# Weights on a second DMA queue, wider pixel loads, and a forward transform split in three frequency ranges, in a convolution kernel

## The chip, the cores and the metric

One NeuronCore of a Trainium2 chip. The metric is the device time of one execution in microseconds (us). Each experiment ran on one chip together with runs of the kernel before, and all comparisons below are of runs in the same (fast) state; only under e10 are its slow runs named too. The experiments ran on several chips, so across experiments the ratios to the kernel before are compared, not the times.

## The reference, cut to what matters

```python
def setup_inputs():
    H = W = 224; C = 96; K = 7
    return {"x": normal(1, H, W, C) * 0.05,      # bfloat16
            "w": normal(K, K, C, C) * 0.05}      # bfloat16

def reference(x, w):
    wp = jnp.pad(w, ((0, H - K), (0, W - K), (0, 0), (0, 0)))
    Xf = rfft2(x.astype(float32), axes=(1, 2))
    Wf = rfft2(wp.astype(float32), axes=(0, 1))
    Yf = jnp.einsum('bhwi,hwio->bhwo', Xf, Wf)
    return irfft2(Yf, s=(H, W), axes=(1, 2)).astype(bfloat16)
```

It is a circular 7x7 convolution of a 224x224 image with 96 channels in and out. The image wraps round, so the first columns need the six last ones; they are called the halo here.

## The kernel before

The kernel transforms along the height only. The 224 rows are cut into 8 blocks of 28, and each block with its 6 rows of overlap (34 rows) goes to 17 frequencies by a matmul with a matrix `Fm` that the kernel computes at its start (iotas, a sine on ScalarE, masks on GpSimd, a cast on VectorE). The width is worked through in 7 tiles of 32 columns, in the order: forward transform (xn by Fm gives xf), one *round* for each of the 17 frequencies (products with the transformed weights WF), inverse transform. Sums and differences of xf (the J buffers) save products. Two tiles run interleaved at first: tile 1 follows tile 0 with a lag of four rounds. The weights are transformed too (wq by Em gives WF): the first group, of two frequencies, in the head and the other five groups during the rounds.

All loads are issued by SyncE, in this order:

```python
load_rows(xh_bufs[0], 0, W - PAD, PAD)     # halo, rows of block group 0: 112 + 6 partitions, 6 pixels
load_x(0)                                  # 16 pixels, 112 + 6 partitions
load_rows(xh_bufs[1], 1, W - PAD, PAD)     # halo of group 1
load_x(1)
for h in range(2):
    if h:
        for c in range(2, NXN):            # NXN = 4 pixel buffers
            load_x(c)
    for p0, p1 in ((0, 48), (48, PW)):     # weights: 48 rows of 18,432 bytes, then the 49th
        dma(wq[h * PW + p0:h * PW + p1, 0:C * C - h * C2], wsrc[p0:p1, h * C2:])
```

ScalarE's program begins with the table load for the sine (a dummy activation), then the sine for Fm. PE warms its clock with 24 matmuls on zeros and then runs the head:

```python
a0 = a_jobs(0)                   # tile 0, whole forward: 12 halo matmuls + 64, all of 136 columns
p0 = prep_jobs(0)                # weights of frequencies 0 and 1: 96 matmuls of 50 columns
for _ in range(16): a0.pop(0)()
for _ in range(4):  p0.pop(0)()
while p0 or a0:                  # the two are mixed
    if p0: p0.pop(0)()
    for _ in range(2):
        if a0: a0.pop(0)()
...
for r in range(NS + LAG):        # rounds
    if r == 0:
        add(0, 2 * LAG - 2, a_jobs(1))   # tile 1's forward beside rounds 0 to 3, 136 columns
```

Each result in PSUM is evicted by ScalarE or VectorE, whichever a running account of their work says is less loaded.

## Time and profile before

| | before |
|---|---|
| median time | 291.92 us (290.88 to 292.42) |
| profiled span | 291.0 us |
| PE busy | 272.5 us, 94% |
| mean granted clock | 0.965 |
| first forward matmul | 8.74 us |
| first weight-transform matmul | 14.54 us |
| first product of round 0 | 26.43 us |
| start of the last group of weight transforms (round 16) | 82.56 us |

In the timeline a row gives the start of a group, its busy time, its engine and line, the operation, and in brackets the idle time before it with what ended it. "SPq" and "ACTq" are the sequencers of SyncE and ScalarE, with the DMA issues. Two things of the kernel before matter later. The first is when its sine runs; the second is that one load already waits. From the timeline of the head:

```profile
3.83 0.64 SPq L86 DMA_DIRECT2D wq<-in_w_dram  x2
5.39 0.41 ACT L86 ACTIVATE ct<-ct,ct 118x136 f32<-118x136 f32 x1 [3.10 <-DVE ct L86]
```

And from the waits of SyncE's queue in the first 40 us (sum of the waits, how many, longest):

```profile
SPq L86 <- DMA wq<-in_w_dram: 5.5, 2, 5.3
SPq L86 <- DMA xn<-in_x_dram: 2.9, 4, 0.9
```

The reader is to see that the sine waited for nothing but VectorE's arithmetic (5.39 us), and that SyncE stood 5.3 us in one wait on a load. SyncE has nothing else to do, so that wait cost nothing. I read it only as a sign of when the weights landed.

### The profile page before, as it was taken

The page shows a single profiled execution, that of the slowest core. Times are in us where ns is not written, and L with a number is a line of the kernel's source. Part 1 is how long each engine was busy: PE and PEld are TensorE (multiplying, and loading weights), DVE is VectorE, ACT ScalarE, POOL GpSimd, SP SyncE. Part 2 cuts the span into 40 slices and gives each one's busy share as a digit, 9 for nine tenths or more (in the row PEclk, how much of TensorE's full clock was granted, in tenths as well). Part 3 has the DMA queues.
Part 4 walks back from the last instruction along what each step waited for, and adds up shares of the span by engine and source line. Part 5 has one row for each costly group of instructions (what it writes and reads, how often), then busy time and mean ns, then how long its engine had stood idle before and what let it go on. Part 6 is the DMA issues. An engine that isn't in the chain of part 4 may idle for free.

```text
span 291.0 us, 11983 instructions
## 1 busy us (share of the span) xinstructions
PE 272.5 (94%) x5010; PEld 244.2 (84%) x5010; DVE 229.6 (79%) x472; ACT 195.8 (67%) x488; POOL 113.1 (39%) x151
## 2 busy tenths in 40 slices
PE   8598998999999998999899998999999999999982
PEld 3488988999999997888899987898988989888761
DVE  7847399997978889979977888787998779786723
ACT  2555994958774555886788867897788865677113
POOL 6824022348446565332643227222552323422100
PEclk9955899999999999999999999999999999999997
DMA  8894142111111299977567685778539543887756
GB/s 195 132 236 124 51 112 84 45 43 44 43 43 49 87 277 193 274 225 216 170 190 206 194 243 144 204 210 237 169 95 267 148 131 108 198 245 197 201 108 189
DMA packets 45830, 46.04 MB, mean 158 GB/s; under 512 B 33626, under 2 KB 34758, under 8 KB 45678
## 3 DMA queue, kind: packets, MB, share of 16 engines
q1 hardware_dynamic: 43488, 43.21, 55.3%
q10 hardware_dynamic: 2288, 2.06, 2.5%
q8 instruction: 39, 0.64, 1.0%
q14 instruction: 15, 0.12, 0.2%
HBM read 23.92 MB, written 21.33 MB: 156 GB/s over the span
## 4 chain that ended last, share of the span: by engine, by line
PE 65%; DVE 14%; DMA 5%; issue 5%; POOL 4%; ACT 4%; SPq 1%; DVEq 0%; ACTq 0%; POOLq 0%
PE pb L86 65%; DVE J L86 6%; POOL ct L86 3%; DVE v L86 2%; DMA tt<-scr 2%; DVE u L86 2%; DMA xf<-scrb 2%; ACT xf L86 2%; DVE WF L86 1%; DVE yf L86 1%; DVE ct L86 1%; ACT WF L86 1%; POOL yf L86 1%; SPq L86 1%; DMA scrb<-yf 1%
## 5 line engine op out<-in xcount | busy, mean ns | idle before, releaser
L86 PE MATMUL pb<-WF,J 96*128 96x96 bf16 x2898 | 169.2, 206 | 2.8 <-DVE J L86 1.4
L86 PEld LDWEIGHTS <-J 96*128 96x128 bf16 (+1 forms) x2910 | 142.9, 98 | 18.5 <-issue 10.1
L86 POOL TENSOR_TENSOR yf<-v,u 128x384 bf16<-128x384 f32 x85 | 83.7, 999 | 144.9 <-issue 97.3
L86 ACT CAST xf<-pb 96x408 bf16<-96x408 f32 (+3 forms) x150 | 68.4, 481 | 11.3 <-PE pb L86 9.2
L86 ACT CAST yo<-pb 84x384 bf16<-84x384 f32 (+1 forms) x144 | 61.4, 481 | 6.4 <-PE pb L86 3.4
L86 DVE TENSOR_TENSOR J<-xf 96x1824 bf16<-96x1824 bf16 (+1 forms) x84 | 64.4, 806 | 0.0
L86 PE MATMUL pb<-WF,xf 96*128 96x96 bf16 x952 | 60.7, 207 | 2.1 <-DVE WF L86 2.0
L86 PE MATMUL pb<-Fm,xn 118*128 118x136 bf16 (+3 forms) x576 | 52.1, 216 | 2.4 <-DVE u L86 1.9
L86 PEld LDWEIGHTS <-xf 96*128 96x128 bf16 x952 | 47.5, 98 | 2.6 <-issue 1.5
L86 PEld LDWEIGHTS <-xn 118*128 118x128 bf16 x576 | 34.3, 100 | 3.8 <-issue 2.9
L86 PE MATMUL pb<-tt,Gm 102*84 102x384 bf16 (+1 forms) x144 | 35.8, 329 | 0.6 <-DVE v L86 0.4
L86 ACT CAST WF<-pb 96x480 bf16<-96x480 f32 (+1 forms) x62 | 30.7, 570 | 5.1 <-PE pb L86 5.1
L86 PE MATMUL pb<-wq 98*128 98x120 bf16 (+1 forms) x336 | 26.5, 234 | 2.3 <-POOL ct L86 2.3
L86 DVE TENSOR_TENSOR J<-J 96x912 bf16<-96x912 bf16 (+1 forms) x42 | 28.3, 674 | 0.0
L86 PEld LDWEIGHTS <-wq 98*128 98x128 bf16 (+1 forms) x336 | 23.8, 152 | 3.8 <-POOL ct L86 2.4
L86 POOL COPY xf<-xf 96x816 bf16<-96x816 bf16 (+3 forms) x16 | 16.7, 1073 | 0.0
L86 DVE TENSOR_TENSOR yf<-v,u 128x384 bf16<-128x384 f32 x27 | 15.5, 575 | 0.9
L86 PEld LDWEIGHTS <-Gm 102*84 102x84 bf16 (+1 forms) x144 | 11.4, 114 | 3.1 <-issue 0.6
L86 PE MATMUL pb<-wu 128*112 128x384 bf16 (+1 forms) x60 | 13.0, 380 | 1.1 <-DVE ct L86 1.1
L86 PEld LDWEIGHTS <-wu 128*112 128x112 bf16 (+1 forms) x60 | 7.3, 124 | 6.4 <-issue 2.5
L86 DVE TENSOR_TENSOR WF<-WF 96x960 bf16<-96x960 bf16 x15 | 11.0, 787 | 0.1
L86 ACT CAST tt<-pb 112x384 bf16<-112x384 f32 x8 | 3.6, 479 | 9.7 <-PE pb L86 9.6
(388 smaller groups left out, 210.2 us busy)
## 6 DMA issues: line engine op xcount, KB each, us to landing
xn<-in_x_dram SPq DMA_DIRECT2D x28, 336.0 KB
scr<-yf SPq DMA_DIRECT2D x30, 288.0 KB
tt<-scr SPq DMA_DIRECT2D x24, 288.0 KB
out_dram<-yo SPq DMA_DIRECT2D x24, 252.0 KB
tt<-scr SPq DMA_DIRECT2D x12, 192.0 KB
out_dram<-yo SPq DMA_DIRECT2D x12, 168.0 KB
out_dram<-tt SPq DMA_DIRECT2D x4, 336.0 KB
scr<-yf SPq DMA_DIRECT2D x6, 192.0 KB
```

The costliest lines, as they stand in the source:

```text
L86: r = fn(*a, **k)
```

## The change

Its intent: start the weights at once, on ScalarE's queue, so that they don't stand behind the pixels; do only what round 0 needs of the forward transform in the head (frequencies 0 to 7 of 17), and push the other two ranges, and tile 1 in three ranges, into later rounds; keep PE's clock up with nine warming matmuls after the halo (17 stand at the start, where 24 did).

```diff
+    x0_bufs = [xn_bufs[0], J_bufs[2][0:R, 0:XW + 32]]        # 32-pixel buffers; tile 0's second in J
...
+    def load_w(h):
+        for p0, p1 in ((0, 48), (48, PW)):
+            SE.dma_start(out=wq[h * PW + p0:h * PW + p1, 0:C * C - h * C2], in_=wsrc[p0:p1, h * C2:])
+    load_w(0)
     load_rows(xh_bufs[0], 0, W - PAD, PAD)
-    load_x(0)
     load_rows(xh_bufs[1], 1, W - PAD, PAD)
-    load_x(1)
-    ... (weights and two more pieces on SyncE)
+    load_x(0, 0)
+    load_x(0, 1)
...
+    warm(8); warm(9)                     # instead of 24 warming matmuls
...
+    SE.copy(out=zw, in_=...)             # ScalarE zeroes the rest of wq, instead of GpSimd
...
-    VE.tensor_copy(out=Fm..., in_=qf[:]) # this cast comes ahead of the masks now
...
-    (head as above)
+    for jg in range(2):
+        for f in a_bank(0, xf0, xh_bufs[jg], 0, 3, jg, 0):   # halo: 12 matmuls
+            f()
+    warm(9)
+    load_x(1, 1)
+    fj = f_jobs(0, 0)                    # first range: 64 columns instead of 136
+    for f in fj[0]: f()
+    load_w(1)
+    for f in prep_jobs(0) + fj[1]: f()
...
-        add(2 * PGRP[gi - 1][0], 2 * PGRP[gi - 1][1] - 1, prep_jobs(gi))
+        add(2 * PGRP[gi - 1][0] + (gi == 1), 2 * PGRP[gi - 1][1] - (gi > 1), prep_jobs(gi))   # weights: group 1 a step later
...
-            add(0, 2 * LAG - 2, a_jobs(1))
+            f1, f2 = f_jobs(0, 1), f_jobs(0, 2)
+            add(0, 4, f1[0] + f2[0][:-1] + [then_load(f2[0][-1], 1, 0)] + f1[1] + f2[1])
+        for p in range(3):
+            if r == (1, 3, 5)[p]:        # tile 1's three ranges
+                new_xf(1, SH2[p], SH2[p + 1])
+                fj = f_jobs(1, p)
+                ...
+                add(2 * r + 1, 2 * r + (5, 5, 4)[p], fj[0] + fj[1])
```

More of the change, by code (lines that the diff above doesn't have):

```diff
@@ L40 @@
 CQ = {2: (12, 0), 3: (12, 2), 4: (10, 5), 5: (7, 8), 6: (4, 12)}
-NXN = 4
 SH2 = (0, 8, 13, 17)
@@ L143 @@
     assert sum(KB) == 128
-    xn_bufs = [cpool.tile([R, PXC * C + 32], BF16, name=f"xn{i}") for i in range(NXN)]
+    XW = 2 * TW * C
+    xn_bufs = [cpool.tile([R, XW + 32], BF16, name=f"xn{i}") for i in range(2)]
+    x0_bufs = [xn_bufs[0], J_bufs[2][0:R, 0:XW + 32]]
     wtmp_cm = tc.tile_pool(name="wtmp", bufs=1, side="right")
@@ L153 @@
     XHW = PAD * C + 32
-    xh_bufs = [J_bufs[2][0:R, i * XHW:(i + 1) * XHW] for i in range(2)]
-    for xb in xn_bufs:
-        GE.memset(xb[:, PXC * C:], 0.0)
+    xh_bufs = [xn_bufs[1][:, i * XHW:(i + 1) * XHW] for i in range(2)]
+    for xb in (xn_bufs[0], xn_bufs[1], x0_bufs[1]):
+        GE.memset(xb[:, XW:], 0.0)
     for xb in xh_bufs:
@@ L167, in load_rows, with xbuf, load_x @@
         ld(0, PAD, h0 % H)
-    def load_x(c):
-        t, k = divmod(c, 4)
-        h, jg = divmod(k, 2)
-        load_rows(xn_bufs[c % NXN], jg, t * 2 * TW + h * PXC, PXC)
+    def xbuf(t, jg):
+        return (xn_bufs if t else x0_bufs)[jg]
+    def load_x(t, jg):
+        load_rows(xbuf(t, jg), jg, t * 2 * TW, 2 * TW)
     wsrc = w.rearrange("kh kw i o -> (kh kw) (i o)")
-    NCH = 4 * NT
+    def load_w(h):
+        for p0, p1 in ((0, 48), (48, PW)):
+            SE.dma_start(out=wq[h * PW + p0:h * PW + p1, 0:C * C - h * C2], in_=wsrc[p0:p1, h * C2:])
+    load_w(0)
     load_rows(xh_bufs[0], 0, W - PAD, PAD)
-    load_x(0)
     load_rows(xh_bufs[1], 1, W - PAD, PAD)
-    load_x(1)
-    for h in range(2):
-        if h:
-            for c in range(2, NXN):
-                load_x(c)
-        for p0, p1 in ((0, 48), (48, PW)):
-            dma(wq[h * PW + p0:h * PW + p1, 0:C * C - h * C2], wsrc[p0:p1, h * C2:])
+    load_x(0, 0)
+    load_x(0, 1)
+    for xf in xf_bufs:
+        GE.memset(xf[0:C, :, :, NS - 1, POS - 1, :], 0.0)
     wu = cpool.tile([128, 128], BF16, name="wu")
@@ L189, with warm @@
     VE.memset(wu[:], 0.0)
-    for _ in range(3):
+    def warm(n):
         pwu = bank()
-        for _ in range(8):
+        for _ in range(n):
             TE.matmul(pwu[:].rearrange("p (a b) -> p a b", a=4), lhsT=wu[:, 0:128], rhs=wur, start=True, stop=True)
+    warm(8)
+    warm(9)
     ntmp = [0]
@@ L212 @@
     SE.activation(out=dmy[:], in_=pi_t[:], func=ACTF.Sin, bias=0.0, scale=0.0)
+    zw = wqx[0:PW2, C * C + 2 * NSLOT * NTAP:]
+    SE.copy(out=zw, in_=wu[0:PW2, 0:1].to_broadcast(list(zw.shape)))
     def sin_q(q):
@@ L230 @@
     iota(twc[:], [[1, KT]])
-    GE.memset(wqx[0:PW2, C * C + 2 * NSLOT * NTAP:], 0.0)
     VE.memset(a2[:, 0, 1:2], 34.0)
@@ L251 @@
     sin_q(qe[:])
+    VE.tensor_copy(out=Fm.rearrange("p r s j -> p j s r"), in_=qf[:])
     VE.tensor_scalar(out=mk[:, 0:KT], in0=twc[:], scalar1=twp[:, 0:1], scalar2=None, op0=ALU.is_equal)
@@ L255 @@
     VE.tensor_tensor(out=mk2[:, 0], in0=mk[:], in1=mk2[:, 1], op=ALU.subtract)
-    VE.tensor_copy(out=Fm.rearrange("p r s j -> p j s r"), in_=qf[:])
     pe3 = ftile([PW2, NSLOT])
@@ L395, in a_bank, with then_load, g @@
         return [pair] if t > 2 and NP2 else [single(0), single(1)]
+    def then_load(f, t, jg):
+        def g():
+            f()
+            if t < NT:
+                load_x(t, jg)
+        return g
     def a_jobs(t):
@@ L399, in a_jobs @@
         jobs = []
-        if t == 0:
-            for jg in range(2):
-                jobs.extend(a_bank(t, xf, xh_bufs[jg], 0, 3, jg, 0))
-        for k in range(4):
-            h, jg = divmod(k, 2)
-            c = 4 * t + k
-            for (q, n) in ((0, 3), (3, 3), (6, 2)):
-                jobs.extend(a_bank(t, xf, xn_bufs[c % NXN], 2 * q, n, jg, HALO + h * 8 + q))
-            last = jobs.pop()
-            def fin(last=last, c=c):
-                last()
-                if c + NXN < NCH:
-                    load_x(c + NXN)
-            jobs.append(fin)
+        for jg in range(2):
+            for h in range(2):
+                for (q, n) in ((0, 3), (3, 3), (6, 2)):
+                    jobs.extend(a_bank(t, xf, xn_bufs[jg], h * PXC + 2 * q, n, jg, HALO + h * 8 + q))
+            jobs.append(then_load(jobs.pop(), t + 1, jg))
         return jobs
@@ L427, in f @@
                 for k in range(b - a):
-                    h, i = divmod(2 * (a + k) + ph, PXC)
-                    xb = xn_bufs[(4 * t + 2 * h + jg) % NXN]
-                    TE.matmul(pa[:, k * n:(k + 1) * n], lhsT=xb[:, i * C:i * C + 128], rhs=fv, start=True, stop=True)
+                    i = 2 * (a + k) + ph
+                    TE.matmul(pa[:, k * n:(k + 1) * n], lhsT=xbuf(t, jg)[:, i * C:i * C + 128], rhs=fv, start=True, stop=True)
                 xo = xf_tiles[t][0:C, ph, :, s0:s1, HALO + a:HALO + b, jg * JG:(jg + 1) * JG]
@@ L434, in mk_ @@
             return f
-        return [mk_(jg, a, b, ph) for jg in range(2) for a, b in zip(e[:-1], e[1:]) for ph in range(2)]
+        return [[mk_(jg, a, b, ph) for a, b in zip(e[:-1], e[1:]) for ph in range(2)] for jg in range(2)]
     jbuf = {}
@@ L649, in queue_c @@
         pump()
-    a0 = a_jobs(0)
-    p0 = prep_jobs(0)
-    for _ in range(16):
-        a0.pop(0)()
-    for _ in range(4):
-        p0.pop(0)()
-    while p0 or a0:
-        if p0:
-            p0.pop(0)()
-        for _ in range(2):
-            if a0:
-                a0.pop(0)()
+    xf0 = new_xf(0)
+    for jg in range(2):
+        for f in a_bank(0, xf0, xh_bufs[jg], 0, 3, jg, 0):
+            f()
+    warm(9)
+    load_x(1, 1)
+    fj = f_jobs(0, 0)
+    for f in fj[0]:
+        f()
+    load_w(1)
+    for f in prep_jobs(0) + fj[1]:
+        f()
     for f in jit(0, 0):
@@ L706 @@
         if r == 0:
-            add(0, 2 * LAG - 2, a_jobs(1))
+            f1, f2 = f_jobs(0, 1), f_jobs(0, 2)
[4 more added lines that the diff above has]
+                fj = f_jobs(1, p)
+                if p == 2:
+                    for jg in range(2):
+                        fj[jg][-1] = then_load(fj[jg][-1], 2, jg)
+                add(2 * r + 1, 2 * r + (5, 5, 4)[p], fj[0] + fj[1])
         for p in range(3):
@@ L712 @@
                 if p == 2:
-                    for i in (1, 3):
-                        def fin(f=fj[i], i=i):
-                            f()
-                            for h in range(2):
-                                load_x(12 + 2 * h + i // 2)
-                        fj[i] = fin
-                add(2 * r, 2 * r + (8, 7, 5)[p], fj)
+                    for jg in range(2):
+                        fj[jg][-1] = then_load(fj[jg][-1], 3, jg)
+                add(2 * r, 2 * r + (8, 7, 5)[p], fj[0] + fj[1])
         if r == PGRP[-2][1] + 1:
```

## The prediction

> **What bounds the kernel now.** I read the page first: PE is busy 94% of the span, and the row of the granted clock shows one hole.
>
> ```profile
> PE   8598998999999998999899998999999999999982
> PEclk9955899999999999999999999999999999999997
> ```
>
> Each digit is a slice of 7.28 us. PE works in every slice after the head, but in slices 3 and 4 its clock is near one half. The diff touches the first two tiles only, so next I read the timeline of 0 to 45 us.
>
> ```profile
> 8.22 0.47 DVE L86 CAST Fm<-ct 118x136 bf16<-118x136 f32 x1
> 8.74 0.87 PE L86 MATMUL pb<-Fm,J 118*128 118x136 bf16 x12 [0.70 <-DVE ct L86]
> ...
> 14.32 28.73 SPq L86 DMA_DIRECT2D xn<-in_x_dram  x16
> 14.54 2.50 PEld L86 LDWEIGHTS <-wq 49*128 49x128 bf16 x40 [2.43 <-POOL ct L86]
> ...
> 18.51 0.86 PE L86 MATMUL pb<-Fm,xn 118*128 118x136 bf16 x6
> ...
> 19.30 0.71 PE L86 MATMUL pb<-wq 49*128 49x50 bf16 x8
> ...
> 26.43 0.80 PE L86 MATMUL pb<-WF,xf 96*128 96x96 bf16 x8 [0.75 <-DVE WF L86]
> ```
>
> Here the reader sees the head: the forward transform waits for the matrix Fm (8.7 us), the weight transform waits until 14.5 us, and the first product of the convolution comes at 26.4 us. The wait of 2.4 us before 14.54 is put down to GpSimd, but the only GpSimd write that those matmuls read, a memset, ended at 4.4 us. SyncE's queue was released at the same moment (14.32), and the waits of that queue name the weight DMA with 5.3 us. So I take it that the first half of the weights landed at about 14.2 us, although it was issued at 3.8, behind 0.97 MB of pixels.
>
> Then the windows of ten microseconds:
>
> ```profile
> 20.00:30.00 10.00, 9.25 (x98) 8.16 (x98) 7.01 (x10) 6.06 (x15) 3.02 (x3) 0.50 0.53 133
> 30.00:40.00 10.00, 9.68 (x156) 9.09 (x154) 5.30 (x10) 9.64 (x26) 0.00 (x0) 0.91 0.29 76
> 50.00:60.00 10.00, 10.00 (x217) 10.00 (x216) 9.22 (x19) 7.41 (x17) 4.64 (x5) 1.00 0.09 33
> ```
>
> The columns are PE, PEld, DVE, ACT, POOL, then clock, DMA share and GB/s. From 30 to 40 us ACT is full (9.64), from 50 us on PE is. I count rounds by the products on xf: round 1 starts at 33.4, 2 at 37.0, 3 at 42.2, 4 at 45.1 us. So there are three stages: a head to 26.4 us that waits and runs at half clock; rounds 0 to 3 (18.7 us) bound by ACT's evictions; and from round 4 on PE.
>
> Last, what a matmul costs in a dense stream, read from the starts of successive groups on PE:
>
> ```profile
> 69.65 0.40 PE L86 MATMUL pb<-Fm,xn 118*128 118x64 bf16 x8
> 69.88 0.93 PE L86 MATMUL pb<-WF,J 96*128 96x96 bf16 x18
> ...
> 76.98 0.92 PE L86 MATMUL pb<-wq 98*128 98x120 bf16 x12
> 77.73 0.40 PE L86 MATMUL pb<-Fm,xn 118*128 118x64 bf16 x8
> ...
> 89.57 0.36 PE L86 MATMUL pb<-Fm,xn 118*128 118x40 bf16 x8
> 89.78 1.16 PE L86 MATMUL pb<-WF,J 96*128 96x96 bf16 x18
> ...
> 108.04 0.34 PE L86 MATMUL pb<-Fm,xn 118*128 118x136 bf16 x3
> 108.22 0.33 PE L86 MATMUL pb<-WF,J 96*128 96x96 bf16 x4
> ```
>
> 77.73 - 76.98 over 12 is 62 ns for a weight transform; (89.78 - 89.57)/8 is 26 ns for 40 columns; (108.22 - 108.04)/3 is 60 ns for 136. (69.88 - 69.65)/8 is 29 ns for 64 columns, in a group that nothing stalls; 16 of 32 columns take 0.40 us, 25 ns. The weight transform took 62 ns at half clock too (2.50 us of weight loads for 40), so it is bound by its strided weight loads and not by the clock.
>
> **What the Trainium skill says.** "TensorE: Matmul & The Clock Gate", section "What's actually happening": PE is half rate by default, a busy window of 3413 ns frees it, an idle one throttles it, and windows run free. The trace agrees: weight loads of the warm-up come every 0.43 us to 4.4 us and every 0.21 after; the half clock lasts from about 14.6 to 31.7 us (from the 0.66 and 0.57 of two 2 us windows), 17.1 us or five such windows. It also shows that a busy PE isn't enough: the mixed stream of 14.6 to 28 us didn't bring the clock back. "DMA: Bandwidth & Descriptors", section "Issuing engines are not separate DMA queues": issuing from two engines "will only save the time on the sequencer". The same page, "Queues, rings and completion order": an engine takes turns between the queues' rows packet by packet. So ScalarE's queue adds no bandwidth, but the weights no longer stand behind the pixels. No trace of the kernel before shows two busy queues in the head.
>
> **The change part by part.**
>
> 1. *Fm.* Its cast moves ahead of the mask work on VectorE and can start near 7.5 instead of 8.22 us; two more GpSimd memsets cost about 0.15. First forward matmul at about 8.2 us: 0.5 gained.
>
> 2. *Weights on ScalarE's queue.* They now start at about 1 us with the halos. By 14.2 us the old head had moved some 2.3 MB, 190 GB/s. Weights (0.88 MB) and as much of the pixels at that rate, from 2 us on, is 11 us (estimate; I allow 9.5 to 13).
>
> 3. *Forward of tile 0 in the head.* Instead of 76 matmuls of 136 columns, 12 for the halo and 64 of 64 columns for the first range; 17 warming matmuls at first and 9 more after the halo. From 8.2 us: 12 x 60 ns = 0.7; 9 x 213 ns = 1.9 (the old warm-up's spacing); 32 x 29 ns = 0.9; 96 x 62 ns = 6.0; 32 x 29 ns = 0.9; last eviction and hop 0.8 as before. That sums to 11.2, so the first product comes at 19.4 us, and with half a microsecond for a late landing at 19.9. Against 26.4: **6.5 us gained**. The weights are wanted at 11.7 us, just after my estimate of their landing.
>
> 4. *Rounds 0 to 3.* Out go 24 evictions of tile 1 (16 of 408 columns at 0.48 us, 8 of 272 at 0.38: 10.7 us). In come 12 of tile 0's ranges two and three (8 of 320 at 0.42, 4 of 512 at 0.61: 5.8) and 10 of tile 1 (8 of 512, 2 of 320: 5.7): 11.5 us. Weight evictions are unchanged. ACT stays the bound and has 0.8 more, halved by the balance with VectorE, so 18.7 becomes about 19.1. The end of the half clock changes little where ACT is the bound. **0.4 lost.**
>
> 5. *Rounds 4 to 7.* The rest of tile 1 falls where PE is full: 48 x 26 ns + 64 x 25 ns = 2.85 us. Some may fill the 1.3 us that PE waits for the weight differences at 49.2 us: I take **2.3 lost**.
>
> 6. *The rest.* From round 9 the program is the same apart from 32-pixel loads, which have over 4 us of slack. Nothing.
>
> Sum: 6.5 - 0.4 - 2.3 = 3.8 us. A count by PE alone agrees: it loses the wait of 2.2, about 4.4 of half clock (32 of 136 columns at 133 instead of 60 ns, and 2 us in the rounds) and 1.5 in the first forward stage, gains 1.9 of warming and two times 1.3 of splitting (64 x (29+26+25) ns = 5.1 against 3.8): 3.6. Part of the splitting lies in the ACT-bound rounds and is free, so I add a little: 4.4 us, **287.5 us**.
>
> **The rivals.**
>
> *The clock falls anyway.* The weight transform now runs in one block with 50 columns in 62 ns, 21 ns of array work, a third. The window before 14.6 us, with about a quarter of work, lost the clock; the one to 11.2 us, with half, kept it. A third is between. If it falls at about 18 us, the first rounds run at half clock as now and the gain shrinks by 1 to 2: 289 us.
>
> *The weights are still late.* They fill only 48 partitions and the rate fell to 70 to 130 GB/s between 9 and 13 us while they were in flight. Landing at 14 again would take 2.3 us: 290 us. Against it: they start 3 us earlier and have a queue of their own.
>
> *ACT binds the early rounds harder.* The evictions start with a bias of 8 us towards ACT; in rounds 0 and 1 all 24 (12.6 us) may go there while VectorE idles. That costs 1 to 2: 289 us.
>
> *The relief is larger than counted.* VectorE idled some 5 us in rounds 0 to 3, waiting on a slow PE. With full clock these rounds may shrink by 2 to 3 us and round 5's wait vanish: 284 us.
>
> **Range and chances.** The gains are of the head and certain in sign; the give-backs are about half as large. One rival coming true costs 1 to 2.5 us, two leave almost nothing; the good one brings 3. So 283.8 to 290.6 us. Faster by over 2% needs under 286.1 us, 1.4 below my figure: 0.3. Slower by over 2% would need a new long wait: 0.02.
>
> **What would show it.** The first product of weights and xf should lie near 19.9 us; the first weight transform near 12 us without a wait; the clock at one from 4.4 us on (a half from about 18 is rival one); round 4 near 39 us; and the lead over the kernel before should fall from over 6 us at round 4 to about 4 at round 8 and stay. If the lead doesn't fall, step 5 is wrong and those rounds weren't bound by PE; if it is small at the first product, step 2 is.

## The result, and the profile after

The changed kernel took 300.83 us (median, 299.65 to 301.50) against 291.74 us of the kernel before in the same rounds. The ratio is 1.031, with a 95% interval of 1.027 to 1.035: slower by 3.1%, where 287.5 us was predicted. A ratio here is the mean time of one kernel's fast runs over that of the other's fast runs of the same rounds, so not quite the ratio of the quoted medians.

The page of the changed kernel has these rows of tenths, one digit for each of 40 slices of 7.5 us:

```profile
PE   7079899899999998999999998999999999899972
PEclk9857699999999999999999999999999999999999
```

Compared with the rows of before, the second digit of PE has become 0: from 7.5 to 15 us PE did next to nothing. The timeline of the first 36 us says why:

```profile
0.80 10.83 ACTq L85 DMA_DIRECT2D wq<-in_w_dram  x2
...
3.22 8.43 SPq L85 DMA_DIRECT2D J<-in_x_dram  x2
...
11.67 1.28 ACT L85 ACT_TABLE_LOAD   x1 [11.67 <-DMA wq<-in_w_dram]
...
13.07 1.90 ACT L85 COPY wq<-wu 98x2072 bf16<-98x2072 bf16 x1
14.88 0.62 ACT L85 ACTIVATE ct<-ct,ct 118x136 f32<-118x136 f32 x2
...
16.10 0.47 DVE L85 CAST Fm<-ct 118x136 bf16<-118x136 f32 x1 [9.76 <-POOL ct L85]
...
16.62 1.52 PE L85 MATMUL pb<-Fm,xn 118*128 118x136 bf16 x12 [9.68 <-DMA J<-in_x_dram]
...
17.94 4.04 PE L85 MATMUL pb<-wu 128*128 128x512 bf16 x9
...
21.78 1.34 PE L85 MATMUL pb<-Fm,xn 118*128 118x64 bf16 x32
...
23.05 6.08 PE L85 MATMUL pb<-wq 49*128 49x50 bf16 x96
...
32.46 0.82 PE L85 MATMUL pb<-WF,xf 96*128 96x96 bf16 x8 [0.35 <-DVE xf L85]
```

The first row is the one to learn from. Two DMA issues on ScalarE took from 0.80 to 11.63 us, though one issue takes 0.4 us: the first was done at 1.23 us, and the second began at 11.16. ScalarE's first own instruction, the table load, comes at 11.67 and was released by the weight load. The table load and the zeroing copy (1.90 us), which the change moved to ScalarE, then still ran ahead of the sine. So the sine ran at 14.88 instead of 5.39 us, Fm was cast at 16.10 instead of 8.22, and the first forward matmul came at 16.62 instead of 8.74.

The bracket of the matmul row names the pixel load `J<-in_x_dram` with 9.68 us. That is misleading: those 12 matmuls read xn and Fm, not J. The chain of waits that ended last repeats it:

```profile
0.81 10.56 DMA xn<-in_x_dram
...
11.38 5.22 DMA J<-in_x_dram
```

A reader who stops here would blame the pixels for 16 us. The cast of Fm, 16.10 to 16.57 us, ended just ahead of the matmul at 16.62, so Fm was the last input to come.

Why the second issue waited stands in the order of the program. This listing shows the first instructions of ScalarE and SyncE in the changed kernel, with the semaphores that each waits for (read from the built program; it is not a view of the profile):

```
ACT  1 DMACopy wq<-in_w_dram 48x9216
     2 DMACopy wq<-in_w_dram 1x9216 [waits DMAHW0_49]
     3 LoadActFuncSet
     4 Activation ct_120<-ct_118 128x1 [waits DVE_49]
     5 TensorCopy wq<-wu 98x2072
     6 Activation ct_145<-ct_145,ct_118 118x136 [waits DVE_49]
SP   1-4 DMACopy xn_72<-in_x_dram 112x576, 6x576, 112x576, 6x576
     5 DMACopy xn_71<-in_x_dram 112x3072
     6 DMACopy xn_71<-in_x_dram 6x3072
     7 DMACopy J_66<-in_x_dram 112x3072
     8 DMACopy J_66<-in_x_dram 6x3072 [waits DMAHW1_49]
```

Eight loads wait for nothing (seven on SyncE, one on ScalarE); the next two wait for DMAHW0 and DMAHW1. The program gives its loads eight completion semaphores in turn, whichever engine issues them, and a ninth load must wait until the one that had its semaphore has landed. The ninth is the one row of weights left over from 48, and behind it, in ScalarE's own program, stands the sine. Its semaphore, DMAHW0, is that of the first load, the 48 rows: ScalarE waited for its own first load. The packed trace agrees: the last of the 16 increments of that semaphore came at 11.14 us, and the second issue began at 11.16. The 49th row itself then landed at 17.38 us.

| us | before | predicted | after |
|---|---|---|---|
| Fm cast | 8.22 | 7.5 | 16.10 |
| first forward matmul | 8.74 | 8.2 | 16.62 |
| first weight-transform matmul | 14.54 | 11.7 | 23.05 |
| first product of round 0 | 26.43 | 19.9 | 32.46 |
| start of round 4 | 45.11 | 39 | 51.45 |
| start of round 8 | 60.36 | | 69.17 |
| last group of weight transforms | 82.56 | | 90.37 |
| span | 291.0 | | 299.8 |

The rounds are compared by windows between the same products. The columns are those explained in the prediction. First the kernel before, rounds 0 to 3, rounds 4 to 7, and the sum of the three windows from 26.43 to 82.56 us:

```profile
26.43:45.11 18.68, 18.35 (x281) 17.61 (x282) 13.54 (x24) 16.60 (x41) 4.68 (x4) 0.86 0.34 95
45.11:60.36 15.25, 13.99 (x304) 13.88 (x303) 14.47 (x27) 9.56 (x23) 5.93 (x6) 1.00 0.11 39
...
sum 56.13, PE 53.42 PEld 52.16 DVE 47.08 ACT 42.56 POOL 22.25; mean PE 17.81 PEld 17.39 DVE 15.69 ACT 14.19 POOL 7.42
```

Then the changed kernel, the same rounds and the sum from 32.46 to 90.37 us:

```profile
32.46:51.45 18.99, 18.37 (x425) 18.17 (x426) 14.47 (x25) 17.30 (x41) 5.46 (x7) 0.91 0.19 58
51.45:69.17 17.72, 16.82 (x421) 16.70 (x417) 15.77 (x29) 12.41 (x31) 7.61 (x8) 1.00 0.34 94
...
sum 57.91, PE 55.77 PEld 55.36 DVE 48.66 ACT 46.14 POOL 24.72; mean PE 18.59 PEld 18.45 DVE 16.22 ACT 15.38 POOL 8.24
```

Rounds 4 to 7 grew by 17.72 - 15.25 = 2.47 us, rounds 0 to 3 by 18.99 - 18.68 = 0.31, and the later ones to the last weight transform shrank by 1.0. So 6.0 us of the 8.8 us by which the profiled spans differ are there at the first product, 1.8 come in the rounds, and 1.0 in the rest (tiles 2 to 6 and the tail), which I didn't follow further: from the last weight transform to the end the kernel before took 208.4 us, and e3, e10 and e12, whose program is the same there, took 206.7 to 207.6, so kernels that do the same work differ by more than that.

### The profile page after: what moved, and what is told of

Its sections match the earlier page's. It is cut to its first block, busy times and chain, and to the rows that moved or that the text cites. A ratio compares the mean times of both kernels' runs of the same rounds, so it can differ in the third digit from the quotient of the medians.

```text
span 299.8 us, 12457 instructions
## 1 busy us (share of the span) xinstructions
PE 273.2 (91%) x5268; PEld 246.2 (82%) x5268; DVE 226.2 (75%) x466; ACT 197.9 (66%) x487; POOL 113.6 (38%) x155
## 4 chain that ended last, share of the span: by engine, by line
PE 62%; DVE 14%; DMA 14%; issue 4%; POOL 2%; ACT 2%; DVEq 0%; SPq 0%; ACTq 0%
PE pb L85 62%; DMA xn<-in_x_dram 7%; DVE J L85 6%; DVE v L85 3%; DMA tt<-scr 2%; DVE WF L85 2%; DVE yf L85 2%; DVE u L85 2%; DMA J<-in_x_dram 2%; DMA xf<-scrb 2%; POOL xf L85 1%; DMA scrb<-yf 1%; ACT xf L85 1%; POOL yf L85 1%; DVE xf L85 0%
## 5 line engine op out<-in xcount | busy, mean ns | idle before, releaser
L85 PEld LDWEIGHTS <-J 96*128 96x128 bf16 (+1 forms) x2994 | 145.3, 98 | 16.9 <-issue 10.3
L85 ACT CAST xf<-pb 96x408 bf16<-96x408 f32 (+3 forms) x148 | 70.1, 491 | 15.3 <-PE pb L85 13.2
L85 DVE TENSOR_TENSOR J<-xf 96x1824 bf16<-96x1824 bf16 (+1 forms) x84 | 63.1, 790 | 0.4 <-ACT xf L85 0.4
L85 PE MATMUL pb<-Fm,xn 118*128 118x136 bf16 (+3 forms) x748 | 50.8, 200 | 12.6 <-DMA J<-in_x_dram 9.7
L85 PEld LDWEIGHTS <-xn 118*128 118x128 bf16 x748 | 35.3, 99 | 14.0 <-DMA xn<-in_x_dram 7.2
L85 PE MATMUL pb<-wq 98*128 98x120 bf16 (+1 forms) x336 | 24.6, 228 | 0.0
L85 PEld LDWEIGHTS <-wq 98*128 98x128 bf16 (+1 forms) x336 | 22.7, 154 | 0.1
L85 POOL COPY xf<-xf 96x816 bf16<-96x816 bf16 (+3 forms) x20 | 18.0, 930 | 0.0
L85 PE MATMUL pb<-wu 128*112 128x384 bf16 (+1 forms) x62 | 15.9, 424 | 1.1 <-DVE ct L85 1.1
L85 DVE TENSOR_TENSOR yf<-v,u 128x384 bf16<-128x384 f32 x27 | 15.3, 567 | 0.9
L85 DVE TENSOR_TENSOR WF<-WF 96x960 bf16<-96x960 bf16 x15 | 11.2, 797 | 0.0
L85 DVE CAST tt<-pb 112x384 bf16<-112x384 f32 x8 | 4.2, 554 | 8.8 <-PE pb L85 8.5
```

The costliest lines, as they stand in the source:

```text
L85: r = fn(*a, **k)
```

## The experiments

The theories, with the letters that the expectations use: **A**, ScalarE is held by its second weight load, because of the eight semaphores, and everything behind the sine is late. **B**, the halo pixels are late because they share the DMA engines with the long packets of the weights: in the trace of the changed kernel the 236 halo packets of 1,152 bytes ended at 10.67 us, against 4.92 in the kernel before, while each weight packet of 18,432 bytes held an engine for 1.74 us. From 5 to 7 us 14 halo packets and 16 weight packets went, which fits queues that take turns packet by packet. **C**, splitting the forward transform costs more than its gain in the head. **E**, which came later: weights land late because their packets are long. A rival to A was that ScalarE's queue as such is slow to issue. All twelve kernels gave correct results.

| kernel | median us | ratio to before (95%) | first forward | first product | last weight transform |
|---|---|---|---|---|---|
| before | 291.7 to 292.1 | 1 | 8.74 | 26.43 | 82.56 |
| after | 300.83 | 1.031 (1.027 to 1.035) | 16.62 | 32.46 | 90.37 |
| e1_row_on_sync | 295.26 | 1.012 (1.007 to 1.016) | 10.83 | 26.79 | 84.71 |
| e2_weights_on_sync | 293.65 | 1.006 (1.004 to 1.009) | 7.47 | 25.41 | 83.70 |
| e3_before_scalar | 296.37 | 1.016 (1.014 to 1.018) | 14.89 | 31.09 | 87.06 |
| e4_scalar_later | 296.57 | 1.014 (1.008 to 1.020) | 10.81 | 27.00 | 85.30 |
| e5_pixels_first | 291.22 | 0.997 (0.996 to 0.999) | 6.82 | 23.76 | 81.99 |
| e6_tile1_ranges | 294.50 | 1.009 (1.006 to 1.012) | 8.79 | 26.45 | 84.38 |
| e7_small_packets | 292.28 | 1.002 (0.999 to 1.004) | 7.17 | 24.22 | 82.56 |
| e8_prep_first | 291.34 | 0.997 (0.994 to 1.000) | 6.82 | 22.75 | 81.23 |
| e9_wide_prep | 293.30 | 1.003 (1.000 to 1.005) | 6.82 | 24.00 | 83.29 |
| e10_before_clock | 292.66 | 0.999 (0.996 to 1.002) | 8.75 | 28.61 | 84.49 |
| e11_thirds_first | 290.79 | 0.996 (0.993 to 0.998) | 7.36 | 21.32 | 79.85 |
| e12_before_thirds | 291.36 | 0.998 (0.995 to 1.000) | 8.74 | 26.02 | 82.25 |

### The held engine

**One row of weights back on SyncE** (the changed kernel otherwise):

```diff
-    load_w(0)                            # both loads on ScalarE
+    load_w(0, ((0, 48),))                # 48 rows on ScalarE
     load_rows(xh_bufs[0], 0, W - PAD, PAD)
     load_rows(xh_bufs[1], 1, W - PAD, PAD)
+    load_w(0, ((48, PW),), DE)           # the 49th row on SyncE
```

> The changed kernel, but the one-row weight load is issued by SyncE, so that ScalarE's queue holds only the first weight load, which waits for nothing. Theory A (ScalarE stood from 1.2 to 11.2 us before its second weight load, which waits for a completion slot, and the sines behind it came 9.5 us late): the sine of the forward matrix runs near 5 us instead of 14.9, and Fm is cast near 7.5-8 us. If A is the whole loss, the first forward matmul comes at 8.2 us and the time falls to about 289 us. Theory B (the halo pixels land at 11.4-11.9 us because 18 KB weight packets alternate with their 1152-byte packets): the first forward matmul still waits for the halo, near 11.8 us, PE is cold by then, and the time is about 296 us. Rival C (the ranges and 32-pixel pieces are what costs): no change from 300.8.

It took 295.26 us. From the timeline of its first 18 us:

```profile
0.80 0.43 ACTq L85 DMA_DIRECT2D wq<-in_w_dram  x1
...
6.27 0.46 DVE L85 CAST Fm<-ct 118x136 bf16<-118x136 f32 x1
...
10.83 1.54 PE L85 MATMUL pb<-Fm,xn 118*128 118x136 bf16 x12 [3.21 <-DMA xn<-in_x_dram]
```

Moving one load of 18 KB brought Fm from 16.10 to 6.27 us, the first product from 32.46 to 26.79, and the time from 1.031 to 1.012 of the kernel before. That is A, and it is 5.7 us of the loss (1.0309 - 1.0115, of 291.9 us). Now the halo matmuls wait truly for their pixels until 10.83 us, 4.1 us after Fm was there: that is B.

**Only the first half of the weights on ScalarE, in the kernel before:**

```diff
+    for p0, p1 in ((0, 48), (48, PW)):
+        SE.dma_start(out=wq[p0:p1, 0:C * C], in_=wsrc[p0:p1])
     load_rows(xh_bufs[0], 0, W - PAD, PAD)
```

> The kernel before with one part of the change alone: the first half of the weights on ScalarE's queue ahead of everything. A: its second load waits for a slot until about 11 us, the first forward matmul comes near 16 us instead of 8.7, the wait for weights at 14.5 vanishes: 8 us lost, about 3 gained back, 296-299 us. Rival C: not slower than 292, or a little faster, since weights come early.

It took 296.37 us, as expected. From its timeline:

```profile
0.80 10.91 ACTq L86 DMA_DIRECT2D wq<-in_w_dram  x2
...
14.36 0.47 DVE L86 CAST Fm<-ct 118x136 bf16<-118x136 f32 x1 [6.11 <-POOL ct L86]
```

The hold appears without any other part of the change (10.91 us in two issues), and the kernel is 1.6% slower, whatever the earlier start of the weights gained. Here the awaited semaphore is that of a six-row halo load, which landed at 11.21 us; the issue began at 11.23.

**Both weight loads on ScalarE, but written after its zeroing copy:**

```diff
-    load_w(0)                            # ahead of everything
...
     SE.copy(out=zw, in_=...)
+    load_w(0)
```

> The changed kernel with the weight loads still on ScalarE's queue, but issued after its zero copy at about 5 us, ahead of the two sines; by then the halos have landed and slots are free. A and B: no block, Fm near 8.2 us, halos by 5 us, first product near 21 us, total about 289 us. If weights beside pixels on two queues are slow for themselves (theory B for the 6 KB pixel rows), the first range waits for pixels: 291-293.

This missed: 296.57 us, with 289 expected. (Its interval straddles 2%, and the profiled run had a dip of the clock at 110.7 to 114.1 us.) The timeline of ScalarE:

```profile
1.06 0.39 ACTq L85 DMA_DIRECT2D wq<-in_w_dram  x1
...
8.55 0.47 ACTq L85 DMA_DIRECT2D wq<-in_w_dram  x1
9.07 0.62 ACT L85 ACTIVATE ct<-ct,ct 118x136 f32<-118x136 f32 x2 [4.97 <-DMA xn<-in_x_dram]
```

The first issue went out at 1.06 us although the copy written ahead of it runs at 2.20: the sequencer doesn't wait for the engine to finish before it issues. But the second still waits for its semaphore, till 8.55, and the sine behind it till 9.07. I had moved the loads behind the copy and forgotten that the sine comes after both. The miss supports A: whatever stands behind a waiting issue is held.

The rival, a queue on ScalarE that is slow as such, falls with e7 below, where two loads that wait for nothing went out on it back to back from 0.80 to 1.70 us. Which load was awaited differs, as the trace's semaphores show: the 48 rows of weights in the changed kernel, the first six-row halo load on SyncE in e3 and in e4 (landed at 8.53 us there, issue at 8.55). The hold isn't tied to one load, but to the load eight places before.

### The order of pixels and weights

**All loads on SyncE; halo, weights, then pixels:**

```diff
-            SE.dma_start(out=wq[...], in_=wsrc[...])
-    load_w(0)
+            DE.dma_start(out=wq[...], in_=wsrc[...])
     load_rows(xh_bufs[0], 0, W - PAD, PAD)
     load_rows(xh_bufs[1], 1, W - PAD, PAD)
+    load_w(0)
     load_x(0, 0)
```

> The changed kernel with all weight loads on SyncE, after the halos and before the other pixels; nothing is issued on ScalarE. A and B together: halos land by 5 us, Fm near 8, first forward matmul near 8.2, first product near 20-21 us, rounds as in the changed kernel (267.3 us from the first product to the end): about 288 us. Rival C: still near 300.

It took 293.65 us where 288 was expected. The first forward matmul came at 7.47 us, better than predicted for the change, and the halo packets ended at 3.48, so both A and B were out of the way. Then PE stood again, as its timeline shows:

```profile
15.31 1.87 PE L85 MATMUL pb<-Fm,xn 118*128 118x64 bf16 x32 [5.02 <-DMA xn<-in_x_dram]
```

The last packet of the weights had ended at 11.34 us, as my estimate said, but the first 32-pixel piece, which the first range needs, landed only at about 15.2.

**The first piece ahead of the weights:**

```diff
     load_x(0, 0)
+    load_w(0)                            # on SyncE
     load_x(0, 1)
```

> The changed kernel with all loads on SyncE in the order halos, first 32-pixel piece, weights, second piece: about the order of the kernel before. If the order of the loads is what is left of the loss (theory B), the first range's matmuls run by 12 us, the weights land near 14-15 us as before, the weight transform takes 6 us, the first product comes near 23 us, and with 266 us from there to the end the time is 289-290. If the rounds' splitting (C) is what is left, it comes near 293.5 like the run with the weights first.

This took 291.22 us, a little above what was expected. Its wait has changed places:

```profile
15.54 6.04 PE L85 MATMUL pb<-wq 49*128 49x50 bf16 x96 [4.97 <-DMA wq<-in_w_dram]
```

Both must be there before PE can go on, and together they take 15 us of landing in either order. In the kernel before this time is covered: it has a 16-pixel piece at 8.7 us and transforms whole pixels while the weights arrive.

**The weight transform first, the first range mixed into its end** (e2 and this):

```diff
-    for f in fj[0]: f()
-    for f in prep_jobs(0) + fj[1]: f()
+    pj = prep_jobs(0)
+    for f in pj[:8]: f()
+    for i in range(4):
+        fj[0][i](); pj[8 + i]()
+    for f in fj[1]: f()
```

> As the run with the weights on SyncE, but PE does the weight transform (weights land at 11.4 us) before the first range's forward, whose pixels land at 15.3, the last four jobs interleaved. If the head is bound by what lands when (theory B), the wait of 5.0 us falls to about 1, the first product comes near 20.5-21 instead of 25.4 and the time is 287.5-289. If not, 293.5 as before.

It took 291.34 us. The transform started at 11.99 us after a wait of 2.36 for the weights, and the first product came at 22.75 us, 3.7 us ahead of the kernel before. But at the last weight transform only 1.3 us of that lead are left (81.23 against 82.56), and the time missed the expectation of 287.5 to 289 us. (This profiled run had a clock dip at 106.6 to 110 us, after that point.)

**Short packets.** In the changed kernel, with the 49th row on SyncE, the 48 rows were loaded in thirds of their columns, 6,144 bytes a packet:

```diff
+    def third(eng, c0):
+        eng.dma_start(out=wq[0:48, c0:c0 + c3], in_=wsrc[0:48, c0:c0 + c3])
+    third(SE, 0)
+    third(SE, c3)
     load_rows(xh_bufs[0], 0, W - PAD, PAD)
     load_rows(xh_bufs[1], 1, W - PAD, PAD)
+    third(DE, 2 * c3)
```

> As the run with the one-row load on SyncE, but the 48 weight rows in three loads of 3072 columns (6 KB packets), two on ScalarE and the third on SyncE after the halos. Theory B (packets of the two queues alternate one for one, so the halo's 14 packets an engine wait for as many weight packets): with weight packets a third as long the halo lands near 6 us instead of 10.2, and the first forward matmul comes at 7.5-8 instead of 10.8. Rival (the halo is slow because the bytes of the weights share the rate, whatever the packets): it lands near 10 us again.

(The 49th row goes on SyncE after the first pixels.) It took 292.28 us. The halo packets ended at 7.52 us instead of 10.2 in e1, so less of the delay went than expected. That doesn't show that the length of the packets counts, for the edit also took a third of the weights off ScalarE's queue: 96 packets of 6,144 bytes are left on it, 0.59 MB, where e1 had 48 of 18,432, 0.88 MB. They ended at 6.90 us here and at 9.49 in e1, which is about 120 GB/s in both, and the halo ended 0.6 to 0.7 us later in both. So the halo came when the weights on the other queue were through; whether their packets are short or long no run tests with the same bytes. The expectation's "as many weight packets" was miscounted as well: with turns one for one, 48 or 96 weight packets are through before 236 halo packets are.

**The same thirds in the kernel before, alone:**

```diff
-            dma(wq[h * PW + p0:h * PW + p1, 0:C * C - h * C2], wsrc[p0:p1, h * C2:])
+        for c in range(3):
+            a, b = c * (n // 3), (c + 1) * (n // 3)
+            dma(wq[h * PW:h * PW + 48, a:b], wsrc[0:48, h * C2 + a:h * C2 + b])
```

> The kernel before with one edit: both halves of the weights in three loads each. Theory E: the first half lands near 11.5 us instead of 14.2, PE's wait of 2.2 us at 12.3 vanishes, the clock doesn't fall at 14.6, and the time is 287.5-290. Rival: weights at 14 us, 291-292.

It took 291.36 us, the same within the interval, and the transform started at 14.29 instead of 14.54 us. So E mostly falls. (Landings scatter, too: in e10, with the loads of the kernel before, the transform started only at 15.98 us.)

### What the splitting costs

**Only tile 1's forward in three ranges, in the kernel before:**

```diff
     if r == 0:
-        add(0, 2 * LAG - 2, a_jobs(1))
+        pass
+    for p in range(3):
+        if r == (1, 3, 5)[p]:
+            new_xf(1, SH2[p], SH2[p + 1])
+            fj = f_jobs(1, p)
+            ...
+            add(2 * r + 1, 2 * r + (5, 5, 4)[p], fj)
```

(The zeroing of one corner of xf that this needs is in the run as well, and so is the change's shift of the second weight group by one step, so the two are not told apart.)

> The kernel before with one part of the change alone: tile 1's forward in three ranges over later rounds; the head untouched. Predicted terms: rounds 0 to 3 lose 14 of 24 evictions of tile 1 (about 5 us of ScalarE and VectorE together, so up to 2.5 us shorter), rounds 4 to 7 gain 2.85 us of matmuls: 291-292.5 us. If the splitting is what costs in the rounds beyond that (C), 294.

It took 294.50 us, slower by 0.9%. The head is the same (first product at 26.45), so the windows to the last weight transform can be laid beside those above. Rounds 0 to 3, rounds 4 to 7, and the sum with the third:

```profile
26.45:44.70 18.25, 16.44 (x297) 16.02 (x298) 11.39 (x19) 14.06 (x32) 4.86 (x6) 0.83 0.08 30
44.70:62.94 18.24, 16.92 (x420) 16.69 (x416) 16.57 (x30) 12.54 (x32) 7.61 (x8) 1.00 0.32 93
...
sum 57.93, PE 54.14 PEld 53.28 DVE 46.63 ACT 42.99 POOL 24.11; mean PE 18.05 PEld 17.76 DVE 15.54 ACT 14.33 POOL 8.04
```

In all, 57.93 against 56.13 us is 1.80 lost, and the changed kernel, which moves tile 0's later ranges too, lost 57.91 - 56.13 = 1.78. Rounds 4 to 7 have 420 - 304 = 116 more matmuls, 2.93 us more of PE (25 ns each) and last 2.99 us longer: there PE is the limit and every moved matmul is paid in full. Rounds 0 to 3 lost 2.5 us of ScalarE's work and 1.9 us of PE's and shrank by only 0.43 us. So the moved work had been almost free where it was. This is C, shown by this part alone (with the shift of the weight group). It also corrects my reading of rounds 0 to 3: evictions on ScalarE (14.06 of 18.25 us here) can't be all that bounds them.

### The clock

The prediction gave 4.4 us of PE time to the clock. It stood at half in the changed kernel from 12.06 to 22.3 and from 25.7 to 35.96 us, and it fell in every profiled run. In three the fall came after 3.4 us in which matmuls of the forward and the weight transform filled PE without a gap: the changed kernel at 25.7, e1 at 20.25 and e3 at 22.30 us. In others PE stood waiting just before (e2 at 13.45, e5 at 14.76 us, and the changed kernel's first fall at 12.06), or had waited for part of the 3.4 us (e8 at 14.45 us).

**e8 with the transform streaming its columns twice, and ten more warming matmuls ahead of it:**

```diff
-  TE.matmul(pv_[:, k], lhsT=wqx[0:PW, o:o + 127 * C + 1:C], rhs=ev, ...)
+  TE.matmul(pw[:, k * ncol:(k + 2) * ncol]..., lhsT=wqx[0:PW, o:o + 127 * C + 1:C],
+            rhs=ev.unsqueeze(1).to_broadcast([PW, 2, ncol]), ...)
...
+    warm(10)
```

> As the run with the weight transform first, and the clock kept up: the transform's matmuls stream their 50 columns twice (100 columns, 42 ns of array work beside a weight load of 62 ns; the second copy is overwritten by the next matmul), and ten more warming matmuls fill PE until the weights land. Theory D (the half clock from 14.5 to 28 us costs time: 32 matmuls of 64 columns at 77 instead of 29 ns in the interleaved part, as many at 59, and the first rounds): the clock stays at 1, the first product comes at 20.5-21 instead of 22.75 and the total falls by 2-3 us to 288-289. Rival (the head is bound by landings and evictions, not by the clock): within half a microsecond of 291.

It took 293.30 us, a miss: the clock fell at 14.64 us all the same, and at half clock the wider matmuls cost 0.88 instead of 0.68 us for eight.

**The same two things in the kernel before** (eleven warming matmuls in the wait for the weights):

```diff
+    pwu = bank()
+    for _ in range(11):
+        TE.matmul(pwu[:]..., lhsT=wu[:, 0:128], rhs=wur, start=True, stop=True)
```

> The kernel before with the clock kept up alone: 11 warming matmuls in its wait for the weights at 12.3-14.5 us and the same doubled columns in the weight transform. My prediction's count by PE said the half clock costs 4.4 us. Theory D: the clock stays at 1 to the first product, which comes near 24 us instead of 26.4, and the total is 287.5-289. Rival: evictions of ScalarE bind rounds 0 and 1 anyway, so only the 2.4 us of the head remain or less: 289.5-291.

It took 292.66 us in the median of all its 20 runs, and the ratio of the fast ones shows no change. But the runs differ among themselves. Two had a mean clock of 0.997 and one of 0.999, and took 290.05, 290.10 and 289.22 us; two had 0.986 (289.35 and 290.37); the other fifteen had 0.967 to 0.979 and took 291.25 to 296.61, six of them long enough to count as the slow state. Against the median of the kernel before (292.01 us) the three runs of full clock are 1.9 to 2.8 us shorter, and against the median of this version's own nine fast runs of 0.979 and less (292.6) 2.5 to 3.4. So a full clock goes with some 2 to 3.4 us here, not 4.4, though nothing was done to these runs to set it apart, and this version doesn't secure it.

### The best version

**e8 with the weights in thirds, and the second half of the weights loaded ahead of tile 1's pixels:**

```diff
+        for c in range(3):
+            dma(wq[h * PW:h * PW + 48, a:b], wsrc[0:48, h * C2 + a:h * C2 + b])
...
     warm(9)
+    load_w(1)
     load_x(1, 1)
```

> As the run with the weight transform first, all loads on SyncE, but each half of the weights in three loads of 6 KB packets and the second half of the weights ahead of tile 1's pixels. In the run with small packets 0.86 MB moved in 4.9 us (175 GB/s); with 18 KB packets the weights alone took 7.5 us. Theory E (large weight packets are slow to move, and that is what holds the head): the weights land near 8.5-9 us instead of 11, the first product comes near 19-20 instead of 22.75, and the time is 287-289. Rival (48 partitions are slow to write whatever the packets): weights at 11 us, 291 again.

It took 290.79 us (292.12 for the kernel before in the same call), 0.996 of it with an interval below one: a real gain, but of 1.3 us, and within 2% the same. Against the changed kernel it is 0.9955 / 1.0309 = 0.966. Its weights could be used at 10.60 us:

```profile
10.60 4.04 PE L85 MATMUL pb<-wq 49*128 49x50 bf16 x64 [0.42 <-DMA wq<-in_w_dram]
```

That is the landing that the prediction had estimated, 9.5 to 13 us. It is 1.4 us earlier than in e8; by the semaphores the 48 rows landed 0.5 us earlier (10.28 us, 10.74 in e8), and the single 49th row, the last to come in both, 1.4 us (10.46 and 11.85). The first product came at 21.32 us, 5.1 ahead of the kernel before; at the last weight transform 2.7 are left. The expected 287 to 289 us were not reached in the median, though the profiled run's span was 287.2.

## Why the prediction was wrong

**The step that failed is the first term: Fm at 7.5 us and the first forward matmul at 8.2.** They measured 16.10 and 16.62, because ScalarE, which computes the sine for Fm, stood until 11.16 us in its second weight issue. Of the 12.6 us between the predicted first product (19.9) and the measured one (32.46) the terms have these shares:

| term | predicted us | measured us | off by |
|---|---|---|---|
| first forward matmul | 8.2 | 16.62 | +8.4 |
| 12 halo matmuls | 0.7 | 1.3 | +0.6 |
| 9 warming matmuls | 1.9 | 3.84 | +1.9 |
| first range, first half | 0.9 | 1.27 | +0.4 |
| weight transform | 6.0 | 6.0 | 0 |
| late landing | 0.5 | 0 | -0.5 |
| second half and hop | 1.7 | 3.4 | +1.7 |

- *Fm.* I counted what moved within VectorE's program and never wrote down ScalarE's new program in order. The two weight loads stand ahead of the sine in it, and the second waits for the first. The sign was in what I had read: SyncE's wait of 5.3 us on a load was there, and I used it only to date the landing; its four waits on pixel loads (2.9 us) were there too, and in the trace they end when the load eight places ahead has landed (at 5.10 us, issue at 5.12; at 8.26, issue at 8.27). The prediction's "slower by over 2% would need a new long wait: 0.02" names the right condition. What it lacked was the question who executes the wait. The run e1 shows this as the larger part, 5.7 us, and e3 shows the hold alone. With ScalarE free, Fm came earlier than predicted (6.27 us in e1): three VectorE operations on its way took 1.92 us in the kernel before, while GpSimd zeroed part of wq beside them, and 0.76 us where ScalarE zeroes it. I didn't test that alone.
- *Weights on ScalarE's queue.* The landing estimate (9.5 to 13 us) held for the 48 rows, about 11.1 us, and not for the 49th, which every matmul of the weight transform reads too: issued only after the wait, it landed at 17.38 us, so the weights of this kernel were not usable at 11.7. What the second queue takes from the first wasn't counted: the halo's packets were late by 5.7 us (10.67 against 4.92), which e1 shows as a wait of its own once Fm is early. And the step priced only the weights. The first range also needs a 32-pixel piece, and e2 and e5 show that the two together take until 15.3 to 15.5 us. Without the held engine the first product came at 25.41 and 23.76 us there, not at 19.9; the best run reached 21.32 by another order. (The prediction's 0.97 and 0.88 MB are the profile's KB of 1,024 bytes by the thousand; they are 1.00 and 0.90 MB, which moves its landing estimate by some 0.2 us.)
- *The clock* was the first rival and came true in part: its fall in the weight transform came, at 25.7 us, and the second half of the first range ran at half clock. The earlier half clock, in which the nine warming matmuls ran (3.84 us), was none of that rival's: PE had stood idle to 16.62 us. The weight transform took 6.0 us either way, as the 62 ns said. The gain of 4.4 us that the count by PE gave to the clock was probably too large: e10's runs of full clock suggest 2 to 3.4.
- *Rounds 0 to 3*: 0.4 predicted, 0.31 measured, and ScalarE had 0.70 us more work (17.30 against 16.60) where 0.8 was predicted; but e6 above shows that its evictions aren't all that bounds them, so the agreement is in part luck. *Rounds 4 to 7*: 2.3 predicted, 2.47 measured: here the mechanism was right too, and e6 shows with tile 1's ranges (and the shift of the weight group) that the give-back is the change's own. A term that was left out goes the other way: 1.0 us gained from round 8 to the last weight transform.
- *The rest, "nothing"*: 1.0 us more, not explained.

The balance itself was sound only in its second half. With the held engine gone and the loads in the best order tried (e11) the head gains 5.1 us and the rounds to the last weight transform take 2.4 back (the part split in e6 cost 1.8 there). I haven't shown which cause limits what remains.

## What to carry to other kernels

A DMA issue that may wait belongs on a queue with nothing behind it; before moving one to a computing engine, write down that engine's whole program in order and ask of every issue what it waits for, the limited completion semaphores included. Order loads by first use and add up what must have landed before each stage: a second queue changes who waits, and a small load on one queue may land only when a large one on the other is through. Splitting work to fill a head is paid for where it is put back, so see first whether that place is full.

## What the Trainium skill lacked or had wrong

- "DMA: Bandwidth & Descriptors", section "Issuing engines are not separate DMA queues", says a second engine only saves the issue's time on the sequencer. It lacks the cost: an issue that waits holds the engine's own program. ScalarE stood from 1.2 to 11.2 us here, and e3, with that part alone, was 1.6% slower. The page has the ground for it in "Anatomy of one DMA — SWDGE (gpsimd) path" (a semaphore wait happens on the issuing sequencer before dispatch), but doesn't join the two; that a program may give its loads only eight completion semaphores in turn (as this one does), so that a ninth issue waits, no page that I read states.
- The same page, "Queues, rings and completion order": turns between queues packet by packet fit the trace (14 and 16 packets from 5 to 7 us). It lacks what that means for a small load beside a large one: with 0.88 MB of weights on the other queue the halo ended at 10.67 us, with 0.59 MB at 7.52, on a single queue ahead of the weights at 3.5 to 5.0.
- "TensorE: Matmul & The Clock Gate", section "What's actually happening", doesn't say how busy a window must be. PE filled without a gap for 3.4 us, for the most part with weight transforms (50 columns in 62 ns; by the 213 ns of 512 columns, an estimated 21 ns of array work), lost the clock in three profiled runs here (the changed kernel, e1, e3). With twice the columns the mean clock was 0.997 or more in only 3 of 20 runs (e10), and at most 0.982 in e9's 20.
